# Attention and two feed-forward layers on one core: other places for the weight conversions in attention, and less filler a unit up to unit 34

## The chip, the core and the metric

The kernel runs on one core of a Trainium2 chip. The core has TensorE (PE: products into PSUM; its weight loads are shown as PEld), VectorE (DVE), ScalarE (ACT), GpSimd (POOL) and SyncE (SP, which issues most of the transfers). Each engine works through its own instructions in their order, and waits on semaphores for the others. The metric is the time of one execution in microseconds (us), the median of several.

## The reference, cut to what matters

```python
# attention: q, k, v are (4, 8, 576, 64), s is (4, 8, 576)
scores = scale * q @ k.T
bias = minimum(-(cum[:, None] - cum[None, :]), 0)       # cum: running sum of max(s, 0)
attn = softmax(where(causal, -1e9, scores + bias))
x = attn @ v                                            # then as (2304, 512)
# first layer: w_in (512, 2048), w_out (2048, 512)
h = x @ w_in ;  x = (h * sigmoid(1.702 * h)) @ w_out
# second layer, weights of its own
h = x @ w_in ;  x = (P(h) / (Q(h) + 1e-6)) @ w_out      # P, Q: polynomials of h and |h|
```

[...]

## The kernel before, in words

**Attention** is cut into 80 units: 4 batches, 4 pairs of heads, 5 blocks of 128 query rows. Unit j has batch j // 20, pair (j % 20) // 5 and block (0, 1, 4, 2, 3)[j % 5]; in the names of the rows, s_3_0 is pair 3, block 0. A unit makes its scores on PE for two heads (L251), adds the mask and takes the row minimum on DVE (L285), the exponential on ACT (L292), the reciprocal of the sums on DVE (L300, L301), and scales the rows on POOL (L304). Two or three units later PE transposes them (L323 to L344), ACT or DVE copies them out of PSUM (L348, L351), and PE multiplies with the values (L370). The first two units of a pair also prepare the next pair: transposes (L218), copies on ACT (L176), differences on DVE (L179).

**Filler.** Between these pieces PE gets pieces of the first layer, for one batch at a time (mlp1_first), over the first 5 of the 16 blocks f of the hidden dimension: first products h (L563), their activation (L574, L575, L577, L580), and then second products a (L587), which sum over all 5 blocks f. How much is given to a unit is set by FILL / 20 in planned microseconds. A piece of 6 products is planned at 0.74. The filler of batch 0 opens at unit 23, that of batch 1 at unit 43, that of batch 2 at unit 63; before unit 23 there is none, and a unit gets only a product or so on idle data (L75).

**Conversions.** A weight block is half of an f: half 0 from w_in, half 1 from w_out. Below, c0 to c4 are half 0 of f = 0 to 4, and c5 to c9 half 1 of them; CONV_J says after which unit each is put out. Six more, p0 to p5, for f = 5, 6, 7, are put out after the units AHEAD_J and parked in DRAM. One conversion is a transfer of 512 KB (L493 or L495 on SP), two ACT instructions (L497, L499), three on DVE (L500, L501, L502), an addition on POOL (L504), the high part on ACT (L505), and the low part on POOL (L506); PE multiplies with both parts. The transferred words lie in a slot of the tile stgA: up to unit 23 always slot 2, then slots 0, 1, 2 in turn (staging; `self.stg_free = j > 23`). A transfer waits until the conversion before it in its slot is past L504.

**Order.** PE's order is written out by hand, as the code says it. For the other engines a planner with costs of its own sets the order inside the limits that the code gives (`behind`: not before the exponential and the reciprocal of unit j). After attention come the rest of the first layer and the second layer; the change moves nothing there.

Of the kernel before, what the change touches and what calls it, by code (L numbers as in the profile page):

```python
# [40 lines left out]
EARLY = tuple(range(3, 40, 5))  # L41
PACE = 0.5
AHEAD_F = (5, 6, 7)
AHEAD_J = (35, 39, 43, 47, 51, 55)
FILL = 33.0
AHEAD, AHEAD_0 = 2, 3
COPY_V = ((0, 0), (0, 4))
W2_SLOTS = 7
CONV_J = (9, 12, 15, 18, 20, 22, 24, 26, 28, 30)
CONV = [(f, 0) for f in range(F1)] + [(f, 1) for f in range(F1)]  # L50
STG = 1536
BT_BUFS, G_BUFS = 7, 9
# [3 lines left out]
class Fused:  # L56
# [340 lines left out]
    def attention(self, att, mlp):  # L397
        units = [(b, p, t) for b in range(NB) for p in range(NP) for t in (0, 1, 4, 2, 3)]
        n = len(units)
        self.pairs, self.state = {}, {}  # L400
        self.filler, self.credit = iter(()), 0.0
        self.n_bt = 0
        self.cold, self.idle_bank = True, self.bank("T", "idle")
        self.warm(10)
        nprep = iter(())
        self.sums_load(att)
        ld = self.pair_load(att, 0, 0, True)
        self.sums(att)
        for _ in self.prep(att, 0, 0, ld, True):
            pass  # L410
        start = ld["values"]
        ld = self.pair_load(att, 0, 1)
        start()
        ld["values"]()
        self.store_sums()
        done = 0
        for j in range(n + AHEAD + 1):
            i = max(j - (AHEAD_0 if j < 20 else AHEAD), -1)
            for e in range(done, i):
                for _ in self.unit_transpose(att, units[e]):  # L420
                    pass
                self.unit_values(att, units[e - 1])
            done, k = i + 1, i - 1
            self.stg_free = j > 23
            tr = iter(())
            if j < n:
                b, p, t = units[j]
                idx = j % 5
                if idx == 0 and units[j][1:] != (NP - 1, 0) or (idx == 0 and b + 1 < NB):
                    nprep = self.prep(att, *divmod(b * NP + p + 1, NP), ld)  # L430
            if i >= 0 and i < n and units[i][0] and i % 20 == 1:
                self.filler = chain(self.filler, self.mlp1_first(mlp, units[i][0] - 1))
                self.cold = False
            q = FILL / 20
            if j < n:
                self.unit_scores(att, units[j], 0)
                if j:
                    next(nprep, None)
            self.fill(q / 3, 1)
            if 0 <= i < n:  # L440
                tr = self.unit_transpose(att, units[i])
                next(tr, None)
            if j < n:
                self.unit_scores(att, units[j], 1)
            self.fill(q / 3, j < 4)
            for _ in tr:
                pass
            if j < n and idx == 4:
                for _ in nprep:
                    pass  # L450
                g = b * NP + p + 2
                if g < NB * NP:
                    ld = self.pair_load(att, *divmod(g, NP))
                    ld["values"]()
            if k >= 0:
                self.unit_values(att, units[k])
            self.fill(q / 3, j < 4)
            if j == AHEAD_J[0]:
                self.stg_n, self.stg_k = 0, 2
                buf = self.stg_slot[:, 2 * STG : 2 * STG + 1024].bitcast(F32R)  # L460
                buf = buf.rearrange("p (i f) -> p i f", i=2)
                self.queue = [
                    lambda f=f, half=half: self.park(buf, 1, f, half)
                    for f in AHEAD_F for half in range(2)
                ]
            if j in COEF_J:
                with self.behind(self.tail):
                    if j == COEF_J[0]:
                        self.coefficients()
                    else:  # L470
                        self.nc.scalar.activation(self.cf[:, 6:8], self.cf[:, 4:6], AF.Abs)
            if j in CONV_J or j in AHEAD_J:
                with self.behind(self.tail):
                    self.emit(1)
        for _ in self.filler:
            pass
# [446 lines left out]
```

## Time and profile before

| | |
|---|---|
| median of 3 runs | 1057.89 us (1056.5 to 1062.92) |
| the profiled execution | 1063.09 us, its span 1061.3 us |
| PE busy | 1030.1 us, 97% of the span |
| DVE, ACT, POOL busy | 804.8, 724.1, 315.7 us |
| attention | the first 327 us or so |

The page gives busy times and groups of instructions for the whole span; further views give the same for a stretch, the instructions in order of time, and what each waited for. A "gap" below is idle time of an engine just before an instruction; the arrow names what ended it. PE's ends are modelled, so PE shown as busy may still be slow; its clock is in the windows' rows (1.00 is full speed, 0.50 half).

### The profile page before, as it was taken

What the parts mean: (1) busy time and instruction counts of PE and PEld (TensorE: products, weight loads), DVE (VectorE), ACT (ScalarE), POOL (GpSimd) and SP (SyncE); (2) the same over time, 40 slices, a digit from 0 to 9 for tenths busy, and PEclk for the clock granted to TensorE, in tenths of its full rate; (3) what the DMA queues carried; (4) which work ended last, traced back from release to release, by engine and by line L of the source; (5) the groups of instructions that cost most, each with busy time, mean ns of one, the idle gap of its engine ahead of it and who ended that gap; (6) DMA issues with size and microseconds to landing.
All of it is one profiled execution on the core that took longest, in us unless ns stands there. A gap on an engine that the chain in (4) does not pass through costs nothing.

```text
span 1061.3 us, 19897 instructions
## 1 busy us (share of the span) xinstructions
PE 1030.1 (97%) x7073; PEld 944.9 (89%) x7073; DVE 804.8 (76%) x1874; ACT 724.1 (68%) x1668; POOL 315.7 (30%) x421
## 2 busy tenths in 40 slices
PE   7998999999999899989999999999999999999997
PEld 4766898898999899889999999998999999999996
DVE  6777867766644999786388444898998988989886
ACT  6788978977855675554265234788787777777765
POOL 4445835543420003231001211222222222222222
PEclk8899999999999999999999999999999999999999
DMA  8446465543215648897136546000010010100000
GB/s 183 117 120 171 122 163 146 144 136 84 50 48 223 204 141 285 273 285 246 46 124 209 196 123 241 31 30 31 1 48 13 17 44 1 33 29 1 31 1 30
DMA packets 79755, 117.31 MB, mean 111 GB/s; under 512 B 25728, under 2 KB 63616, under 8 KB 78060
## 3 DMA queue, kind: packets, MB, share of 16 engines
q1 hardware_dynamic: 73288, 96.55, 31.3%
q0 software_dynamic: 6144, 19.19, 5.0%
q8 instruction: 56, 0.92, 0.4%
q14 instruction: 43, 0.35, 0.1%
q10 hardware_dynamic: 224, 0.30, 0.1%
HBM read 75.08 MB, written 32.05 MB: 101 GB/s over the span
## 4 chain that ended last, share of the span: by engine, by line
PE 80%; DMA 7%; ACT 5%; DVE 4%; issue 3%; POOL 1%; SPq 0%; ACTq 0%; POOLq 0%; DVEq 0%
PE h L563 32%; PE a L739 18%; PE a L587 14%; PE s L251 5%; PE O L370 5%; DMA raw<-in_moe_w_out_dram 4%; PE tp L344 3%; DMA stgA<-in_moe_w_in_dram 1%; PE idle L75 1%; DMA raw<-in_moe_w_in_dram 1%; ACT cvx L499 1%; ACT kh L176 1%; PE tk L218 1%; POOL wd L543 1%; DVE cvx L504 1%
## 5 line engine op out<-in xcount | busy, mean ns | idle before, releaser
L563 PE MATMUL h<-x,u 128*128 128x288 f32 x1536 | 233.0, 298 | 7.6 <-DVE g L575 3.8
L587 PE MATMUL a<-gh,u 128*128 128x288 f32 x1024 | 229.8, 299 | 2.3 <-ACT gh L577 2.3
L563 PEld LDWEIGHTS h<-x,u 128*128 128x128 f32 x1536 | 213.0, 189 | 12.6 <-DVE g L575 4.3
L722 POOL TENSOR_TENSOR gl<-u,gh 128x384 fp32r<-128x384 f32 x96 | 105.5, 1099 | 290.3 <-ACT gh L720 261.1
L587 PEld LDWEIGHTS a<-gh,u 128*128 128x128 f32 x1024 | 172.1, 189 | 6.6 <-ACT gh L577 2.5
L563 PE MATMUL h<-y,u 128*128 128x384 f32 x864 | 165.7, 336 | 0.0
L563 PEld LDWEIGHTS h<-y,u 128*128 128x128 f32 x864 | 152.9, 188 | 6.2
L587 PE MATMUL a<-gl,u 128*128 128x288 f32 x512 | 147.7, 295 | 1.0 <-DVE gl L580 1.0
L739 PE MATMUL a<-u,gh 128*128 128x512 f32 x432 | 114.6, 394 | 0.9 <-ACT gh L720 0.9
L304 POOL TENSOR_SCALAR bt<-bt,sm 128x128 f32<-128x128 f32 (+3 forms) x129 | 72.0, 569 | 112.4 <-DVE sm L301 58.0
L574 ACT ACTIVATE g<-h 128x288 f32<-128x288 f32 x128 | 51.4, 406 | 74.7 <-PE h L563 64.3
L648 POOL DMA_DIRECT2D x<-xp x64 | 35.4, 554 | 224.4 <-DVE g L575 95.6
L587 PEld LDWEIGHTS a<-gl,u 128*128 128x128 f32 x512 | 96.3, 188 | 2.1 <-DVE gl L580 1.6
L292 ACT ACTIVATE bt<-bt,mn 128x128 f32<-128x128 f32 (+3 forms) x129 | 74.8, 580 | 29.2 <-DVE mn L285 27.2
L739 PEld LDWEIGHTS a<-u,gh 128*128 128x128 f32 x432 | 80.0, 188 | 14.9 <-ACT gh L720 1.8
L575 DVE SCALAR_TENSOR_TENSOR g<-g,h 128x288 f32<-128x288 f32 x128 | 57.0, 449 | 45.3 <-ACT g L574 44.9
L285 DVE CUSTOM_DVE_ANT_0 bt<-s,mask 128x128 f32<-128x128 f32 (+3 forms) x129 | 62.3, 483 | 36.8 <-PE s L251 30.9
L720 ACT ACTIVATE gh<-u 128x384 fp32r<-128x384 f32 x96 | 50.6, 527 | 57.7 <-DVE u L718 57.6
L251 PE MATMUL s<-k 68*128 68x256 f32 (+2 forms) x192 | 73.4, 387 | 7.3 <-ACT k L176 4.1
L705 ACT ACTIVATE y<-h,cf 128x384 f32<-128x384 f32 x96 | 55.4, 577 | 33.8 <-PE h L563 33.8
L710 DVE SCALAR_TENSOR_TENSOR y<-s,cf,y 128x384 f32<-128x384 f32 x96 | 59.3, 618 | 20.4 <-ACT s L707 19.1
L577 ACT ACTIVATE gh<-g 128x288 fp32r<-128x288 f32 x128 | 55.5, 440 | 28.3 <-DVE g L575 27.4
(117 smaller groups left out, 2112.2 us busy)
## 6 DMA issues: line engine op xcount, KB each, us to landing
raw<-in_moe_w_in_dram SPq DMA_DIRECT2D x24, 512.0 KB
raw<-in_moe_w_out_dram SPq DMA_DIRECT2D x24, 512.0 KB
x<-xp POOLq DMA_DIRECT2D x64, 144.0 KB, 3.1
wd<-park POOLq DMA_DIRECT2D x36, 256.0 KB, 4.5
u<-wd SPq DMA_DIRECT2D x8, 1024.0 KB
x2p<-st SPq DMA_DIRECT2D x32, 144.0 KB
xp<-x2p SPq DMA_DIRECT2D x32, 144.0 KB
xp<-x SPq DMA_DIRECT2D x32, 144.0 KB
```

Of the source, the lines that this page charges most:

```text
L251: nc.tensor.matmul(sc[: c1 - c0, :w], lhsT=q[:, c0:c1], rhs=k[:, j0 : j0 + w], start=m == 0, stop=m == 1,)
L285: nc.vector.tensor_tensor_reduce(bt[:, j0 : j0 + w], sc[:, :w], mask, 1.0, 3.0e38 if i == 0 else mn[:, 0:1], ALU.add, ALU.min, mn[:, i : i ...
L292: ex = nc.scalar.activation(bt[:, :n], bt[:, :n], AF.Exp, bias=mn[:, i : i + 1], scale=-1.0, accum_out=sm[:, col : col + 1],)
L304: nc.gpsimd.tensor_scalar(bt[:, :n], bt[:, :n], inv[:, i : i + 1], 1.0, ALU.mult, ALU.mult)
L563: nc.tensor.matmul(ps_tile, lhsT=u[:, wl, kk * P : (kk + 1) * P], rhs=x(xl, kk), start=(n == 0), stop=(n == 3 * KD - 1),)
L575: nc.vector.scalar_tensor_tensor(g[:, :w], g[:, :w], 1.0, h, ALU.add, ALU.mult)
L577: nc.scalar.activation(gh[:, :w], g[:, :w], AF.Copy)
L587: nc.tensor.matmul(acc, lhsT=u[:, wl, d * P : (d + 1) * P], rhs=g[gl], start=(first and i == 0), stop=(last and i == 2),)
L705: nc.scalar.activation(y, h, AF.Abs, scale=cf[:, 4:5])
L710: nc.vector.scalar_tensor_tensor(y, s, cf[:, 7:8], y, ALU.mult, ALU.add)
L722: nc.gpsimd.tensor_tensor(gl, p, gh.bitcast(F32), ALU.subtract)
L739: nc.tensor.matmul(accs[m], lhsT=g[gl][:, m * P : (m + 1) * P], rhs=u[:, wl, :], start=(f == 0 and i == 0), stop=(f == NF - 1 and i == 2),)
```

## The change

Three tables of numbers change. CONV_J puts the ten conversions of attention at units 8 to 34 where they were at 9 to 30, four and three units apart and then two to three; five of them now fall before unit 23, where six did. AHEAD_J puts each of the six parked ones three units later. FILL_1 gives each unit before unit 35 25/20 = 1.25 planned us of filler in place of 33/20 = 1.65; from unit 35 on it is 1.65 as before. The work is the same, and the order after unit 62 too.

```diff
-AHEAD_J = (35, 39, 43, 47, 51, 55)
-FILL = 33.0
+AHEAD_J = (38, 42, 46, 50, 54, 58)
+FILL, FILL_1 = 33.0, 25.0
...
-CONV_J = (9, 12, 15, 18, 20, 22, 24, 26, 28, 30)
+CONV_J = (8, 12, 16, 19, 22, 25, 28, 30, 32, 34)
...
-            q = FILL / 20
+            q = (FILL_1 if j < 35 else FILL) / 20
```

**SP, units 18 to 21.** The transfers of c3 (the first L493 of each piece below) and c4 (the second), and what stands around them: vn are the values of the pair after the next, kn and qn its keys and queries, k and kh copies of the prepared ones, L495 halves from w_out. Before:

```order
L225 DMA k_0_861<-qs_0_860 64x1152
L493 DMA stgA<-in_moe_w_in_dram 128x4x256
L152 DMA vn_0_840<-in_v_dram 128x4x64 x2
L156 DMA vn_0_840<-in_v_dram 64x2x64
L204 DMA k_1_1120<-rows 4x2304
L145 DMA kn_3_1745<-in_k_dram 96x2x384
L495 DMA stgA<-in_moe_w_out_dram 128x1024
L145 DMA qn_3_1747<-in_q_dram 96x2x384
L225 DMA kh_1_1118<-kh_1_1118 64x1152
L493 DMA stgA<-in_moe_w_in_dram 128x4x256
```

And of the change:

```order
L225 DMA k_0_861<-qs_0_860 64x1152
L152 DMA vn_0_840<-in_v_dram 128x4x64 x2
L156 DMA vn_0_840<-in_v_dram 64x2x64
L493 DMA stgA<-in_moe_w_in_dram 128x4x256
L204 DMA k_1_1120<-rows 4x2304
L145 DMA kn_3_1700<-in_k_dram 96x2x384
L495 DMA stgA<-in_moe_w_out_dram 128x1024
L145 DMA qn_3_1702<-in_q_dram 96x2x384
L225 DMA kh_1_1118<-kh_1_1118 64x1152
L495 DMA stgA<-in_moe_w_out_dram 128x1024
L493 DMA stgA<-in_moe_w_in_dram 128x4x256
```

The transfer of c3 moved behind the three transfers of vn; that of c4 behind one more L495.

**POOL, units 24 to 26.** L304 scales attention's rows (bt), L580 belongs to the filler, L504 and L506 to conversions c5 and c6. Before:

```order
L580 TENSOR_TENSOR gl<-g,gh 128x288
L504 TENSOR_TENSOR stgA<-stgA 128x512 x2
L506 TENSOR_TENSOR u_1_769<-stgA,u_1_769 128x512
L580 TENSOR_TENSOR gl<-g,gh 128x288
L304 TENSOR_SCALAR bt_1_0_0_1414<-bt_1_0_0_1414,sm_1_0_1413 128x128
L304 TENSOR_SCALAR bt_1_0_1_1461<-bt_1_0_1_1461,sm_1_0_1413 128x128
L506 TENSOR_TENSOR u_0_606<-stgA,u_0_606 128x512
```

And of the change:

```order
L304 TENSOR_SCALAR bt_1_0_0_1389<-bt_1_0_0_1389,sm_1_0_1388 128x128
L304 TENSOR_SCALAR bt_1_0_1_1423<-bt_1_0_1_1423,sm_1_0_1388 128x128
L580 TENSOR_TENSOR gl<-g,gh 128x288
L504 TENSOR_TENSOR stgA<-stgA 128x512
L304 TENSOR_SCALAR bt_1_1_0_1483<-bt_1_1_0_1483,sm_1_1_1482 128x256
L304 TENSOR_SCALAR bt_1_1_1_1514<-bt_1_1_1_1514,sm_1_1_1482 128x256
L506 TENSOR_TENSOR u_0_568<-stgA,u_0_568 128x512
```

Before, two conversions stood there together; now one does, and c6 follows three units later.

**PE and ACT, unit 35 of the change.** The last conversion, c9, writes the tile u_4; a are second products. PE:

```order
L344 MATMUL tp_2_2_1_2102<-ident,bt_2_2_1_1959 128x128 x3
L370 MATMUL O_2_0_1977<-pt_2_4_2001,vn_2_1363 64x64 x10
L587 MATMUL a_0_2034<-gh,u_4_1268 128x288
L587 MATMUL a_0_2034<-gl,u_4_1268 128x288
L587 MATMUL a_0_2034<-gh,u_4_1268 128x288
```

ACT, where O is what PE's L370 above writes:

```order
L292 ACTIVATE bt_3_0_1_2091,sm_3_0_2050<-bt_3_0_1_2091,mn_3_0_1_2092 128x128
L380 ACTIVATE x_79<-O_2_0_1977 128x256
L176 ACTIVATE kh_0_2058<-tk_0_1_2070 64x288
L380 ACTIVATE x_79<-O_2_0_1977 128x64
L505 ACTIVATE u_4_1268<-stgA 128x512
```

Before, L505 of c9 stood on ACT in unit 31, ahead of the exponential of unit 32, and PE's three products with that tile in unit 32. Now L505 stands in unit 35 behind two copies of O, and the products right behind the O that these copies read.

## Rows read from the trace of the kernel before

**Rows 1.** The page, busy us (share of the span) and instructions of each engine.

```profile
PE 1030.1 (97%) x7073; PEld 944.9 (89%) x7073; DVE 804.8 (76%) x1874; ACT 724.1 (68%) x1668; POOL 315.7 (30%) x421
```

**Rows 2.** Windows: units 10-22, 23-34, 63-74; filler stream. Columns in the first line.

```profile
core 0: us, PE busy (x) PEld busy (x) DVE busy (x) ACT busy (x) POOL busy (x), PEclk, DMA share, GB/s
42.20:86.83 44.63, 40.69 (x362) 31.08 (x360) 36.04 (x131) 38.38 (x107) 23.45 (x33) 0.92 0.59 158
86.83:141.59 54.76, 51.41 (x435) 44.97 (x433) 40.00 (x126) 46.19 (x124) 36.34 (x44) 1.00 0.49 126
253.56:303.21 49.65, 49.65 (x435) 44.82 (x433) 30.07 (x109) 37.80 (x106) 19.71 (x32) 1.00 0.25 56
500.00:520.00 20.00, 20.00 (x153) 20.00 (x153) 7.30 (x17) 5.56 (x14) 2.16 (x4) 1.00 0.22 68
```

**Rows 3.** Windows of single units without filler: units 12, 17 and 22.

```profile
49.05:53.81 4.76, 4.76 (x33) 3.82 (x29) 3.54 (x12) 3.41 (x9) 2.90 (x6) 0.64 0.88 229
64.02:68.87 4.85, 3.32 (x33) 2.64 (x30) 2.41 (x10) 2.75 (x8) 0.88 (x3) 1.00 0.45 114
83.83:86.83 3.00, 2.98 (x29) 2.16 (x27) 2.11 (x8) 2.48 (x7) 1.25 (x4) 1.00 0.96 293
```

**Rows 4.** Windows of unit 26 and of its twin in batch 3, unit 66.

```profile
101.22:108.70 7.48, 5.36 (x45) 4.12 (x43) 7.32 (x20) 6.81 (x20) 4.74 (x5) 1.00 0.63 175
265.93:270.30 4.37, 4.37 (x44) 4.03 (x42) 3.84 (x13) 4.27 (x16) 1.50 (x3) 1.00 0.32 69
```

**Rows 5.** Timeline of PE: start, us, what; in brackets the gap and its releaser.

```profile
47.73 0.52 PE L344 MATMUL tp<-ident,bt 128*128 128x128 f32 x3 [1.21 <-ACT pt L348]
...
104.52 0.63 PE L344 MATMUL tp<-ident,bt 128*128 128x128 f32 x4 [1.23 <-DVE g L575]
```

**Rows 6.** Timeline of ACT: the first instruction of c2, c3 and c5.

```profile
66.26 0.65 ACT L497 ACTIVATE stgA<-stgA 128x512 int32<-128x512 uint32 x1 [2.06 <-DMA stgA<-in_moe_w_in_dram]
...
76.23 0.68 ACT L497 ACTIVATE stgA<-stgA 128x512 int32<-128x512 uint32 x1
...
96.37 0.66 ACT L497 ACTIVATE stgA<-stgA 128x512 int32<-128x512 uint32 x1 [0.56 <-DMA stgA<-in_moe_w_out_dram]
```

**Rows 7.** Timeline of SP's queue: transfers of c2, c3, vn and c5.

```profile
60.29 0.38 SPq L493 DMA_DIRECT2D stgA<-in_moe_w_in_dram  x1
...
70.94 0.39 SPq L493 DMA_DIRECT2D stgA<-in_moe_w_in_dram  x1
73.64 2.00 SPq L152 DMA_DIRECT2D vn<-in_v_dram  x2
75.69 0.67 SPq L156 DMA_DIRECT2D vn<-in_v_dram  x1
...
92.69 0.35 SPq L495 DMA_DIRECT2D stgA<-in_moe_w_out_dram  x1
```

**Rows 8.** Timeline of POOL and DVE where c5 and c6 meet.

```profile
101.93 1.43 POOL L504 TENSOR_TENSOR stgA<-stgA 128x512 int32<-128x512 int32 x1 [0.96 <-DVE stgA L502]
...
102.14 1.51 DVE L501 TENSOR_SCALAR stgA<-stgA 128x512 int32<-128x512 int32 x1
```

**Rows 9.** Timeline around the end of c9 (L505, L506) and its first use.

```profile
130.59 0.73 ACT L176 ACTIVATE qs<-tq 64x288 fp32r<-64x288 f32 x2
131.21 0.61 ACT L505 ACTIVATE u<-stgA 128x512 fp32r<-128x512 f32 x1
...
132.05 1.28 POOL L506 TENSOR_TENSOR u<-stgA,u 128x512 fp32r<-128x512 f32 x1
...
133.74 0.38 ACT L380 ACTIVATE x<-O 128x256 fp32r<-128x256 f32 x1 [0.15 <-PE O L370]
...
133.99 0.30 PE L587 MATMUL a<-gh,u 128*128 128x288 f32 x1
```

**Rows 10.** Instructions on the tile stgA: ns min/median/max, first and last start.

```profile
L497 ACT ACTIVATE stgA<-stgA x16: 643/665/689, 43.5 to 227.4; 128x512 int32<-128x512 uint32 x16
...
L501 DVE TENSOR_SCALAR stgA<-stgA x16: 416/427/1506, 45.7 to 230.0; 128x512 int32<-128x512 int32 x16
```

## The prediction

> **What bounds the kernel now.** The page comes first: PE is busy for 97% of the span [rows 1], so only a stretch where PE idles or runs slowly has anything to give. The windows show which. From unit 23 to unit 34 batch 1 takes 54.76 us; batch 3 does the same attention and filler, with no conversion beside it, in 49.65 us, all of it with PE busy [rows 2]. So the conversions c4 to c9 cost that stretch 5.1 us, and without them PE bounds it. Of the 5.1, unit 26 alone has 7.48 - 4.37 = 3.11 [rows 4], where PE waits for DVE [rows 5]. Before unit 23 there is no filler to cover a wait: PE is busy for 40.69 of 44.63 us at a mean clock of 0.92, and ACT for 38.38 [rows 2]. Single units show the price. Unit 22 takes 3.00 us; unit 12, with the same block of rows, takes 4.76 at a granted clock of 0.64, a mean of the levels 2.4 and 1.2 GHz, right behind a gap of 1.21 us on PE [rows 3, 5]. Unit 17, the same block again, takes 4.85, because ACT waits 2.06 us for the transfer of c2 [rows 3, 6]. All that the change moves lies ahead of unit 63; what follows shifts with it, one for one.
>
> **The change, part by part.** Nothing is added or removed, so each term is a wait that goes or comes.
>
> *c0, one unit earlier.* Its words are long there. It goes from blocks 3 and 0 to blocks 2 and 3, which have fewer ACT instructions since no pair is prepared. The gap of 1.21 us in unit 11 and the slow unit 12 behind it (4.76 - 3.00 = 1.76) make 2.97 us [rows 3, 5]. ACT is busy for 86% of this stretch [rows 2], so part of c0's ACT time still shows: I take **-2.5** between 0 and -3.0.
>
> *c1 and c2* keep their places on ACT. c2's transfer is still issued behind the transfers ahead of it on SP, so its wait of 2.06 us stays: **0**.
>
> *c3, one unit later, and behind vn on SP.* Before, its transfer was issued at 70.94, and ACT took up c3 at 76.23 with no wait [rows 6, 7]. Now it comes behind the three transfers of vn, which go out from 73.64, when PE has read the old values, to 75.69 + 0.67 = 76.36 [rows 7]. From issue to ACT's start took 66.26 - 60.29 = 5.97 us for c2, and 96.37 - 92.69 = 3.68 for c5, both ended by the landing [rows 6, 7]. So the words land at 80.0 to 82.3 on the old time line. ACT arrives after one more exponential, about 0.7 long (76.9). It waits 3.1 to 5.4 us; behind it stand the copies of the next pair's keys and the copies of transposes that PE needs. c2's wait of 2.06 made unit 17 1.85 longer, 0.9 for each us [rows 3, 6]. That gives 2.8 to 4.9: **+3.8**. Below, it is 0 if the values are read earlier; above, a half clock as in unit 12 adds 1.8: 6.7.
>
> *c4 and the head of the filler.* Of the 5.1 us in units 23 to 34, 2.0 are not in unit 26, and most of these lie where c4 meets the first filler. With c4 alone there and less filler I take **-1.5**, between 0 and -2.0.
>
> *c5 and c6 apart.* They met because c5 still used slot 2 while c6 took slot 0 at once; now c5 has slot 0, three units ahead of c6. Unit 26's 3.11 us is the bound. One conversion still passes there: **-2.1**, between 0 and -3.1. Part of it shows on DVE: L501 took 1.51 us there, and 0.43 in the median, while L504 of the other conversion ran on POOL [rows 8, 10]. The Trainium skill (SBUF — State Buffer, section "SBUF: two separate sides") says that the two engines hold a shared pair of ports by turns, each for a whole instruction; the row agrees. By that rule L304 and L580 of POOL block DVE as well, which the change does not remove; if all of unit 26 were that, this term would be 0 and the sum 2.1 higher.
>
> *Less filler.* Each of the 12 units from 23 to 34 gets 0.4 planned us less, 4.8 in all; a piece of 6 products, planned at 0.74, takes 6 x 20/153 = 0.78 us [rows 2], so 5.1 us of PE work moves to units 35 to 43. By the plan's prices a batch has 29.6 us of filler. Before, it ran out in unit 40, and units 41 and 42 had none; now 15.0 go by unit 34 and the rest ends in unit 43, and batch 1's ends in unit 61, still before unit 63. PE does the same work in the same units 23 to 62, and no idle unit is filled, since 41 and 42 only ran shorter: 0. But ACT's work in units 23 to 34 is 46.19 us [rows 2] and hardly shrinks, since the activations move only within that stretch, while PE needs 49.65 - 5.1 = 44.6. ACT then bounds it, by up to 46.19 - 44.6 = 1.6 us, lost later on PE: **+1.0**, between 0 and 1.6.
>
> *c9 and the second products.* Before, c9's last part ended at 132.05 + 1.28 = 133.33, and the product that reads it started at 133.99: 0.66 us to spare [rows 9]. Now L505 stands behind two copies of O on ACT, and PE's product right behind that O. From the end of O: the copy 0.38, the copy of keys 0.73 / 2 = 0.37, the second copy, with a quarter of the columns, 0.25 at a guess from these, L505 0.61, then L506 1.28 [rows 9], in sum 2.9; two products (0.26) run between, hand-overs add some 0.2. **+2.8**, PE idle. Below, 0 if PE arrives late for another reason; above, 4.2, if L504 (1.43) [rows 8] is late as well. Behind PE wait the scores of unit 36 and all its engines.
>
> *Parked ones.* p0 to p5 keep their four units, beside filler, as c7 to c9 did inside the 2.0 above: 0, give or take 1.
>
> **Sum:** -2.5 + 3.8 - 1.5 - 2.1 + 1.0 + 2.8 = **+1.5 us**. Against the profiled execution (1063.1; span 1061.3) that is 1064.6. It stands 5.2 above the median of the runs, 1057.9; the runs differ by 6.4, so I put the difference on the median: **1059.4 us**, no measurable change (a measurement of this kernel can tell about 1%, 10.6 us).
>
> **The rivals.**
> *The waits that go are not replaced* (faster). c3's words land in time, or PE has enough transposes ahead, and c9's parts are ready since ACT is less crowded. For it: c7 to c9 cost nearly nothing in filled units. Against it: SP's and ACT's orders as printed. -2.5 - 1.5 - 2.1 + 1.0 = -5.1, with the full gains -8.1: 1050 to 1053. Chance 0.27.
>
> *c3 holds c4 up too* (slower). c4 uses the same slot, so its transfer waits for c3's L504. If c3's words land later than about 81.5, 4.6 us behind ACT's arrival, PE idles for over 4 us with no filler, its clock falls as in unit 12, and c4 comes late to the first filler. c3 then costs 4.9 + 1.8 = 6.7 in place of 3.8, c4 gives nothing: +2.9 + 1.5 on top, 1063.8. For it: the gap of 1.21 us was followed by a clock of 0.64 [rows 3, 5]; against: no clock fell behind the gap of 1.23 in unit 26, where there is filler. The Trainium skill (TensorE: Matmul & The Clock Gate, "What's actually happening") has the clock halved where the array has been idle; unit 12 agrees. Chance 0.25.
>
> *The spacing does nothing* (the change does not do what it says): ACT is the bound of these units however the conversions lie, and what one unit saves another loses: 1058. For it: ACT's 86% [rows 2]. Chance 0.10.
>
> **How the numbers follow.** The forecast, gains and new waits about even, has 0.38. The range goes from the full gains without new waits (1057.9 - 8.1 = 1049.8) to the slower rival with c9's upper end (1063.8 + 1.4) and the spread of the runs (some 3): **1049 to 1068**. Faster by over 1% (below 1047.3) needs the full gains and more: 0.06. Slower by over 1% (above 1068.5) needs all upper ends: 0.09. Within 1%: 0.85.
>
> **What would show it.** Right, if in the new trace ACT's first instruction of c3 has a gap of 3 to 5 us that a transfer ends, unit 35 has a PE gap of 2 to 3 us ahead of the products with f = 4, unit 26 is near 4.4 us, units 11 and 12 have neither gap nor half clock, and unit 63 starts within 5 us of 253.56. Wrong at c3, if that gap is under 1 us; wrong at c9, if PE does not idle there; wrong on the filler, if units 23 to 34 take over 51 us without such gaps, or if ACT is not nearly full there.

## The result and the profile after

The changed kernel takes 1068.08 us (median of 9 runs, 1066.67 to 1073.5); the kernel before, on the same chips, 1059.92 (9 runs, 1056.5 to 1063.99). The ratio is 1.0077, with a 95% interval of 1.0057 to 1.0097: about 8 us **slower**. The forecast was no change, 1059.4; the median lies 0.08 us above the upper end of its range (1068). Two executions of one experiment below (all conversions done by unit 30) took 1656 us at a mean clock of 0.556, and are left out of its median and ratio.

The profiled execution of the changed kernel took 1073.5 us (span 1071.7), 5.4 above the median, so single stretches of it are read with care and sizes are taken from the runs. The page, against [rows 1]:

```profile
PE 1034.1 (96%) x7073; PEld 948.0 (88%) x7073; DVE 808.8 (75%) x1874; ACT 723.5 (68%) x1668; POOL 314.8 (29%) x421
```

Same work, PE a little longer. Unit 63 starts at 262.84 where it was 253.56, and behind it every unit takes what it took. So 9.28 of the 10.4 us between the two traces (spans 1071.7 and 1061.3) lie ahead of unit 63. Windows of the changed kernel (columns as in [rows 2]): units 10 to 22, units 23 to 34, units 35 to 42; then units 12, 21 and 26, and two stretches at half clock.

```profile
43.20:91.36 48.16, 41.33 (x362) 30.76 (x360) 36.91 (x133) 37.83 (x107) 23.99 (x34) 0.93 0.61 157
91.36:139.81 48.45, 45.93 (x399) 40.04 (x398) 40.37 (x121) 43.18 (x121) 30.43 (x39) 1.00 0.41 105
139.81:181.58 41.77, 37.57 (x320) 34.18 (x319) 24.08 (x81) 27.75 (x77) 15.92 (x23) 0.92 0.49 139
50.42:53.60 3.18, 3.18 (x34) 2.69 (x30) 2.54 (x11) 3.00 (x9) 2.57 (x6) 1.00 0.98 251
79.20:87.57 8.37, 5.40 (x35) 3.72 (x32) 6.63 (x19) 7.98 (x24) 3.05 (x4) 0.73 0.64 177
102.94:108.26 5.32, 4.19 (x39) 3.29 (x37) 4.68 (x13) 4.99 (x16) 2.98 (x4) 1.00 0.41 112
83.05:89.87 6.82, 5.74 (x29) 4.20 (x28) 5.05 (x17) 5.08 (x16) 3.28 (x4) 0.50 0.78 215
147.90:154.72 6.82, 6.50 (x30) 6.49 (x31) 2.86 (x9) 3.27 (x9) 0.27 (x1) 0.50 0.40 133
```

And units 35 to 42, and unit 21, of the kernel before:

```profile
141.59:172.17 30.58, 30.58 (x294) 27.65 (x292) 22.28 (x75) 25.16 (x73) 13.11 (x18) 1.00 0.56 154
...
79.91:83.83 3.92, 3.42 (x36) 2.62 (x32) 3.76 (x15) 3.82 (x13) 3.29 (x4) 1.00 0.93 290
```

Units 23 to 34 got shorter, 48.45 for 54.76, as less filler would have it. Units 35 to 42 got longer by 11.2. Of that 3.5 are the filler that moved, since the same stretch takes 34.07 where only the filler is changed (below); the other 7.7 lie in units 35 and 36. Unit 21 takes 8.37 where it took 3.92. By stretches, after minus before, from the starts of the units:

| units | forecast | traces | what is seen there |
|---|---|---|---|
| 0 to 10 | 0 | +1.0 | a half clock from 28.43 to 35.26, ahead of all that moved; before, from 29.13 to 32.54 |
| 11 to 22 | -2.5 + 3.8 = +1.3 | +3.5 | c3's wait, and a half clock behind it |
| 23 to 42 | -1.5 - 2.1 + 1.0 + 2.8 = +0.2 | +4.9 | PE waits for c9, and a half clock behind it |
| 43 to 62 | 0 | -0.1 | the parked conversions cost nothing |

**c3.** ACT's first instructions of c2, c3 and c4 in the changed kernel, against [rows 6]:

```profile
67.33 0.67 ACT L497 ACTIVATE stgA<-stgA 128x512 int32<-128x512 uint32 x1 [2.46 <-DMA stgA<-in_moe_w_in_dram]
...
79.47 0.66 ACT L497 ACTIVATE stgA<-stgA 128x512 int32<-128x512 uint32 x1 [3.34 <-DMA stgA<-in_moe_w_in_dram]
...
92.16 0.69 ACT L497 ACTIVATE stgA<-stgA 128x512 int32<-128x512 uint32 x1
```

And SP's queue, against [rows 7]:

```profile
72.22 2.04 SPq L152 DMA_DIRECT2D vn<-in_v_dram  x2
74.30 0.67 SPq L156 DMA_DIRECT2D vn<-in_v_dram  x1
75.08 0.53 SPq L493 DMA_DIRECT2D stgA<-in_moe_w_in_dram  x1
```

The third transfer is c3's, right behind vn; 4.4 us later ACT takes up the words (the 64-bit weights of a block, read as pairs of 32-bit integers), after a wait of 3.34, inside the forecast's 3.1 to 5.4. What the middle of the term left out is the clock: it is 0.50 from 83.05 to 89.87. PE itself idled for no more than 1.69 us at a time in unit 21:

```profile
81.39 0.47 PE L218 MATMUL tq<-ident,qn 96*128 96x96 f32 x3 [1.69 <-DVE mn L285]
```

c4 starts with no wait for its words.

**c9.** PE in unit 35 of the changed kernel, against [rows 9]:

```profile
142.54 0.95 PE L370 MATMUL O<-pt,vn 128*64 128x64 f32 x20
146.76 0.40 PE L587 MATMUL a<-gh,u 128*128 128x288 f32 x1 [3.28 <-ACT u L505]
...
148.22 0.85 PE L587 MATMUL a<-gh,u 128*128 128x288 f32 x2 [0.92 <-POOL u L506]
```

ACT there, and POOL and DVE ahead of the wait of 0.88:

```profile
144.26 0.37 ACT L380 ACTIVATE x<-O 128x256 fp32r<-128x256 f32 x1
144.66 0.43 ACT L176 ACTIVATE kh<-tk 64x288 fp32r<-64x288 f32 x1
145.97 0.22 ACT L380 ACTIVATE x<-O 128x64 fp32r<-128x64 f32 x1 [0.88 <-DVE x L381]
146.09 0.62 ACT L505 ACTIVATE u<-stgA 128x512 fp32r<-128x512 f32 x1
```

```profile
144.17 1.28 POOL L504 TENSOR_TENSOR stgA<-stgA 128x512 int32<-128x512 int32 x1 [0.75 <-ACT pt L348]
...
144.45 1.03 DVE L300 TENSOR_SCALAR sm<-sm 128x2 f32<-128x2 f32 x1
145.51 0.42 DVE L381 TENSOR_TENSOR x<-O,x 128x256 fp32r<-128x256 f32 x1
```

The order is the one forecast: L505 behind both copies of O, the products behind L505 and L506. The two gaps are 4.2 us where 2.8 were forecast. ACT takes up the first copy 0.77 us after the last O (143.49 to 144.26), with other work in between. c9's own L504 runs on POOL from 144.17 to 145.45, and L505 could not have begun before its end. It begins 0.64 us later still, since ACT's second copy waits 0.88 for DVE's L381, which stands behind an L300 of 1.03 us on two columns, beside that same L504 (last section). Then the clock is 0.50 from 147.90 to 154.72, which the term did not hold at all. Units 35 and 36 take 16.47 us here, and 9.70 before with six more second products.

### The profile page after: what moved, and what is told of

Same layout as the page of the kernel before. It is cut to its first block, busy times and chain, and to the rows that moved or that the text cites. A ratio compares the mean times of both kernels' runs of the same rounds, so it can differ in the third digit from the quotient of the medians.

```text
span 1071.7 us, 19895 instructions
## 1 busy us (share of the span) xinstructions
PE 1034.1 (96%) x7073; PEld 948.0 (88%) x7073; DVE 808.8 (75%) x1874; ACT 723.5 (68%) x1668; POOL 314.8 (29%) x421
## 4 chain that ended last, share of the span: by engine, by line
PE 78%; DMA 9%; DVE 4%; ACT 4%; issue 3%; POOL 1%; SPq 1%; ACTq 0%; DVEq 0%; POOLq 0%
PE h L563 31%; PE a L739 18%; PE a L587 13%; PE s L251 5%; PE O L370 5%; DMA raw<-in_moe_w_out_dram 4%; PE tp L344 3%; DMA raw<-in_moe_w_in_dram 3%; DMA stgA<-in_moe_w_in_dram 1%; ACT cvx L499 1%; ACT raw L497 1%; PE tk L218 1%; POOL wd L543 1%; PE tp L323 1%; DMA k<-qs 1%
## 5 line engine op out<-in xcount | busy, mean ns | idle before, releaser
L304 POOL TENSOR_SCALAR bt<-bt,sm 128x128 f32<-128x128 f32 (+3 forms) x129 | 71.6, 566 | 120.8 <-DVE sm L301 62.2
```

What stands on the lines that cost most here:

```text
L304: nc.gpsimd.tensor_scalar(bt[:, :n], bt[:, :n], inv[:, i : i + 1], 1.0, ALU.mult, ALU.mult)
```

## The experiments

Ratios are to the kernel before, run beside each experiment on the same chip; "changed" is 1.0077. Edits are to the changed kernel where nothing else is said. A difference of two ratios carries about 0.0027, or 3 us, either way (the two intervals taken together, an estimate); what is smaller is not told from noise.

### c9 earlier

```diff
-CONV_J = (8, 12, 16, 19, 22, 25, 28, 30, 32, 34)
+CONV_J = (8, 12, 16, 19, 22, 25, 28, 30, 31, 32)
```

> The changed kernel with the last two conversions of attention put out at units 31 and 32 in place of 32 and 34; all else as changed. Theory (waits and clock): the second products of unit 35 then find c9 ready, the gaps of 3.28 and 0.92 us on PE go and so does the half clock of 6.8 us behind them (3.4 us): 7.6 us less than the changed kernel, so about 1060.5, a ratio to the kernel before of 1.000 (0.997 to 1.003); unit 35 takes 5 to 6 us. Rival (the filler that moved is the loss): no change, ratio 1.008, and units 35 to 42 still take near 41 us. Rival (only the wait counts, the clock falls for another reason): 4.2 us less, ratio 1.004.

Measured: 1064.77 us, ratio 1.0056 (1.0036 to 1.0077). A **miss** for the theory's 1.000: 0.0021 better than changed, with intervals that overlap. PE no longer waits for L505, but units 35 and 36 still take 12.61. First the window, then POOL and PE:

```profile
136.93:149.54 12.61, 10.91 (x92) 9.40 (x91) 8.54 (x29) 9.42 (x30) 7.85 (x11) 0.86 0.47 124
```

```profile
136.91 1.30 POOL L504 TENSOR_TENSOR stgA<-stgA 128x512 int32<-128x512 int32 x1 [1.94 <-DVE sm L300]
138.18 1.26 POOL L506 TENSOR_TENSOR u<-stgA,u 128x512 fp32r<-128x512 f32 x1
139.41 0.79 POOL L580 TENSOR_TENSOR gl<-g,gh 128x288 fp32r<-128x288 f32 x1
140.18 2.48 POOL L304 TENSOR_SCALAR bt<-bt,sm 128x384 f32<-128x384 f32 x4
```

```profile
139.49 0.40 PE L587 MATMUL a<-gh,u 128*128 128x288 f32 x1 [0.77 <-DVE sm L300]
140.82 0.55 PE L344 MATMUL tp<-ident,bt 128*128 128x128 f32 x3 [0.92 <-POOL bt L304]
```

With c8 and c9 one unit apart, their POOL parts fall together (L504 is c9's, L506 c8's), ahead of the rows (L304) that PE wants to transpose. A half clock follows here too, from 141.57 to 144.98. One wait has taken the place of another.

### c3 back

```diff
-CONV_J = (8, 12, 16, 19, 22, 25, 28, 30, 32, 34)
+CONV_J = (8, 12, 15, 18, 22, 25, 28, 30, 32, 34)
```

> The changed kernel with c2 and c3 put out at units 15 and 18, as before the change; the transfer of c3 is then issued ahead of vn again. Theory (waits and clock): ACT's wait of 3.34 us for c3 and the half clock of 6.8 us behind it go; unit 21 takes about 4 us in place of 8.4, so 4 to 7 us less than the changed kernel: about 1062.5, ratio 1.001 to 1.004. Rival (c3's wait only takes the place of another, ACT being full up to unit 23): ratio 1.007 to 1.008, and unit 23 still starts near 91. c9's gaps in unit 35 stay by both.

Measured: 1063.25, ratio 1.0029 (1.0011 to 1.0047): 0.0048, or 5.1 us (2.2 to 8.0), better than changed, as the theory had it. The edit moves c2 as well, so this is the price of the two places together. SP and then ACT at c3, unit 21 behind them, and units 35 and 36:

```profile
68.12 0.39 SPq L493 DMA_DIRECT2D stgA<-in_moe_w_in_dram  x1
70.81 0.94 SPq L152 DMA_DIRECT2D vn<-in_v_dram  x2
```

```profile
74.52 0.68 ACT L497 ACTIVATE stgA<-stgA 128x512 int32<-128x512 uint32 x1
```

```profile
78.36:82.18 3.82, 3.28 (x35) 2.58 (x31) 3.67 (x15) 3.75 (x12) 3.31 (x4) 1.00 0.94 296
133.91:150.25 16.34, 12.14 (x93) 11.04 (x91) 9.61 (x28) 9.81 (x28) 7.38 (x10) 0.79 0.46 132
```

With the transfer ahead of vn, ACT has no wait for c3 and unit 21 no loss. This execution has a half clock of its own earlier, from 66.63 to 73.46, behind c2's wait, so the size is taken from the runs. c9's price stays whole, with its half clock (0.79 is the mean of both units): the two losses are separate.

### The filler alone

Against the kernel before:

```diff
-FILL = 33.0
+FILL, FILL_1 = 33.0, 25.0
...
-            q = FILL / 20
+            q = (FILL_1 if j < 35 else FILL) / 20
```

> The kernel before with the one change that units up to 34 get 1.25 planned us of filler in place of 1.65; the conversions and the parked ones as before. Theory (waits and clock): PE does the same work later; units 23 to 34 get shorter by up to 5 us, units 35 to 43 longer by as much; 1060 to 1061.5, ratio 1.000 to 1.002. Rival (the filler that moved is the loss, since ACT and DVE are too full beside it later): ratio 1.005 to 1.008, with gaps on PE in units 35 to 43.

Measured: 1059.96, ratio 0.9999 (0.9984 to 1.0014). The rival is out. Windows: units 23 to 34, 35 and 36, 35 to 42; then units 11 and 12.

```profile
82.78:135.97 53.19, 48.23 (x399) 41.50 (x398) 41.78 (x125) 46.19 (x125) 35.62 (x44) 0.97 0.50 125
135.97:144.74 8.77, 8.77 (x93) 8.13 (x91) 6.89 (x24) 8.06 (x25) 2.08 (x4) 1.00 0.44 119
135.97:170.04 34.07, 34.07 (x320) 31.14 (x319) 23.68 (x82) 26.58 (x75) 14.05 (x21) 1.00 0.62 172
```

```profile
42.99:50.46 7.47, 6.23 (x68) 5.19 (x67) 7.22 (x26) 6.71 (x22) 5.33 (x8) 1.00 0.59 160
```

Two things are to be seen. Units 23 to 34 lost 36 products (435 to 399), some 4.7 us by the 20/153 of [rows 2], and are 1.6 shorter, where a half clock of 3.4 us (the 0.97) took up to 1.7; units 35 to 42 grew by 3.5. The filler went later, and little else. And units 11 and 12, with c0 still at unit 9, take 7.47 here with no half clock, against 9.08 before. The gap ahead of unit 12 is there (1.18 us), the half clock behind it is not: the slow unit 12 of [rows 3] was not a property of that order.

### PE kept busy while it waits for c9

```diff
             if k >= 0:
                 self.unit_values(att, units[k])
+            if j == 35:
+                self.idle_bank = self.bank("T", "idle2")
+                self.warm(15)
```

> The changed kernel with 15 more products on idle data put into PE's order in unit 35, ahead of the second products that wait for c9, so that PE does not idle through that wait (they take about 2 us if PE has nothing else to do). It tells the price of the half clock apart from that of the wait. Theory (waits and clock): the wait stays, the half clock behind it goes, 3 to 3.4 us less than the changed kernel: 1064.7, ratio 1.004 to 1.005. Rival (the clock falls there whatever PE did, or costs nothing since PE was waiting for others): ratio 1.008; if the added products come late and only add work, 1.009 to 1.010.

Measured: 1065.79, ratio 1.0058 (1.0038 to 1.0078): 0.0019, 2.0 us, less than changed, which is within the noise. The ratio lies between the theory's 1.004 to 1.005, inside the interval, and the rival's 1.008, just outside. In the trace the added products take 3.41 us, not about 2 (lines are 3 higher behind the edit):

```profile
143.36 3.41 PE L75 MATMUL idle<-mask 128*128 128x512 bf16 x14
146.75 0.41 PE L590 MATMUL a<-gh,u 128*128 128x288 f32 x1
...
148.19 0.53 PE L590 MATMUL a<-gh,u 128*128 128x288 f32 x2 [0.91 <-POOL u L509]
```

```profile
139.78:153.27 13.49, 12.53 (x107) 9.59 (x106) 9.45 (x28) 9.28 (x28) 6.60 (x9) 1.00 0.53 153
```

The products that read c9 start when they did (146.75 for 146.76), so the wait is the same; but the clock stays at 1.00, and units 35 and 36 take 13.49 in place of 16.47. Of what c9 costs, the clock is 3.0 us in this pair of traces; the runs, with 2.0, do not contradict it and do not show it by themselves. The Trainium skill (TensorE: Matmul & The Clock Gate, "What's actually happening") has the clock halved where the array has been idle; here it fell where PE idled, in two traces, and did not where PE was given idle data, in this trace and the next experiment's, so the traces agree.

### Both waits kept busy

The last edit, and in unit 21:

```diff
                 self.unit_scores(att, units[j], 0)
+                if j == 21:
+                    self.warm(8)
...
                 self.unit_scores(att, units[j], 1)
+                if j == 21:
+                    self.warm(4)
```

> The changed kernel with products on idle data in both places where PE idles: 12 in unit 21, beside ACT's wait for c3, and 15 in unit 35, ahead of the second products that wait for c9. The waits stay; only PE's idling goes. Theory (waits and clock): no half clock behind either wait, unit 21 takes 5 to 6 us in place of 8.4 and units 35 and 36 13.5 in place of 16.5; 1062 to 1063.5, ratio 1.002 to 1.004, so half or more of the loss is the clock. Rival (the clock behind c3's wait costs nothing, since ACT bounds these units): ratio 1.0055 to 1.006, as with the products in unit 35 alone.

Measured: 1063.55, ratio 1.0050 (1.0029 to 1.0071). **Inconclusive**: it lies between the two expectations. In the traces, units 21 and 22 take 9.92 at a clock of 1.00 for 12.13 in the kernel of the last experiment, but that execution, at 1069.03 the longest of the seven, had half clocks earlier, in units 11, 12, 18 and 19. The clock's share in c3's price is not settled.

### c0 alone

Against the kernel before:

```diff
-CONV_J = (9, 12, 15, 18, 20, 22, 24, 26, 28, 30)
+CONV_J = (8, 12, 15, 18, 20, 22, 24, 26, 28, 30)
```

> The kernel before with c0 put out at unit 8 in place of 9, and nothing else. The forecast's term: units 11 and 12 take 2 to 2.5 us less than the 9.1 of before; ratio 0.998. Rival (the half clock in unit 12 came by the run's luck, and the gap of 1.21 us goes only by half): units 11 and 12 take 7.9 us where the clock is full, as in the changed kernel, and in runs without that half clock nothing is gained over before: ratio 0.999 to 1.000.

Measured: 1060.68, ratio 1.0005 (0.9986 to 1.0025). The term of -2.5 us (0.9976) lies outside. Units 11 and 12:

```profile
44.27:52.15 7.88, 6.95 (x68) 5.24 (x67) 7.14 (x28) 7.11 (x22) 5.16 (x8) 1.00 0.73 204
```

That is 0.4 longer than the 7.47 with c0 at unit 9 and a full clock. The forecast took a half clock of one execution for the price of a place.

### Both cured, with the last two conversions one unit apart

```diff
-CONV_J = (8, 12, 16, 19, 22, 25, 28, 30, 32, 34)
+CONV_J = (8, 12, 15, 18, 22, 25, 28, 30, 31, 32)
```

> The changed kernel with both of the two edits tried alone so far: c2 and c3 put out at units 15 and 18 (c3's transfer ahead of vn), c8 and c9 at 31 and 32. Theory (waits and clock, the two are all of the loss that is left): their gains add up, 2.2 and 5 us by the ratios, so ratio 1.0077 - 0.0048 - 0.0021 = 1.001 (0.999 to 1.003); unit 35 still takes some 8 us, since POOL's second part of c9 stands ahead of the rows that PE transposes there. Rival (one hides behind the other): ratio 1.003 to 1.005.

Measured: 1064.13, ratio 1.0043 (1.0016 to 1.0070). This is in the rival's range, and the theory's 1.001 lies outside; but that 1.001 is itself a sum of three measured ratios, so whether the edits add up is not settled. Units 23 to 34 take 48.81 us, unit 35 still 8.60, by the same collision on POOL as with c9 earlier.

### All conversions done by unit 30

First with the changed filler, and then with the full one as well (the last two lines):

```diff
-CONV_J = (8, 12, 16, 19, 22, 25, 28, 30, 32, 34)
+CONV_J = (8, 12, 15, 18, 22, 25, 27, 28, 29, 30)
...
-FILL, FILL_1 = 33.0, 25.0
+FILL, FILL_1 = 33.0, 33.0
```

> The changed kernel's filler and parked conversions, c0 at 8, c4 at 22 and c5 at 25 as changed, but c2 and c3 at 15 and 18 and c6 to c9 at 27, 28, 29, 30, so that c9 is done three units ahead of unit 35. Theory (waits and clock): the gains of the change are kept (c0, c4, and c5 apart from c6) and neither wait is there; unit 35 near 4.7 us as with the filler alone, unit 63 starts 2 us ahead of that kernel's 251.3; 1057 to 1059, ratio 0.997 to 0.999. Rival (four conversions in four units fill ACT and DVE and cost what the two waits cost): ratio 1.001 to 1.004, with gaps on PE in units 27 to 32.

> The same places of the conversions as in the run that ends them at 30 (c0 at 8, c2 and c3 at 15 and 18, c4 at 22, c5 at 25, c6 to c9 at 27 to 30), the parked ones as changed, but with 1.65 planned us of filler a unit from unit 23 on as before the change. By the theory that less filler is worth nothing by itself: within 0.002 of the ratio of that run. Rival (with full filler the second products begin in unit 32 and wait for c9, whose last part stands in unit 31): gaps of 1 to 3 us on PE in units 32 to 34, ratio 0.002 to 0.004 higher.

Measured: 1064.00, ratio 1.0038 (1.0019 to 1.0057), and 1061.94, ratio 1.0011 (0.9993 to 1.0030). The **rival** was right for the first. Units 35 and 36 take 8.76 with no gap, so c9 in time costs nothing there; but unit 31 takes 10.58:

```profile
115.57:126.15 10.58, 7.30 (x44) 5.95 (x43) 9.81 (x24) 8.67 (x23) 10.58 (x11) 0.71 0.52 137
136.93:145.69 8.76, 8.76 (x92) 8.12 (x91) 6.65 (x25) 7.07 (x24) 2.09 (x4) 1.00 0.46 119
```

```profile
120.87 0.58 PE L251 MATMUL s<-k 68*128 68x256 f32 x1 [2.46 <-DVE k L179]
```

POOL is busy for the whole of it, DVE's differences (L179) of the next pair's keys are late for PE, and the clock is 0.50 from 120.03 on. With full filler the same unit took 8.78 us at full clock, and the rival's wait does not show: PE has no gap over 0.4 us in units 32 to 34. The two ratios differ by 0.0027, the wrong way for the rival and more than the 0.002 of the theory; that is at the edge of the noise, and stays open.

### The second products later

```diff
-FILL, FILL_1 = 33.0, 25.0
+FILL, FILL_1 = 33.0, 22.0
...
-CONV_J = (8, 12, 16, 19, 22, 25, 28, 30, 32, 34)
+CONV_J = (8, 12, 15, 18, 22, 25, 28, 30, 32, 34)
...
-            q = (FILL_1 if j < 35 else FILL) / 20
+            q = (FILL_1 if j < 36 else 38.0 if j < 43 else FILL) / 20
```

> The changed kernel with c2 and c3 at units 15 and 18, all other conversions as changed (c9 at 34), and the filler cut to 1.10 planned us a unit up to unit 35 and raised to 1.90 in units 36 to 42, so that the second products begin in unit 36 and the ones that read c9 come some two units later. Theory (waits and clock): no gap behind L505 or L506 any more; units 35 and 36 take 8 to 9.5 us together; unit 43 starts near 168 to 170; ratio 0.997 to 1.000. Rival (the conversions cost PE the same wherever they lie, and what the spacing saves up to unit 34 is lost to ACT and DVE behind it): ratio 1.002 to 1.004.

Measured: 1059.18, ratio 0.9992 (0.9974 to 1.0011). Against c3 back, which has the same places of the conversions, it is 0.0037 (3.9 us, 1.2 to 6.6) faster. c9's L505 now ends at 140.84 and L506 at 142.21; PE's first product that reads c9 starts at 141.82 and the one that needs L506 at 142.26, just in time, since products that read other tiles fill units 35 and 36:

```profile
140.92 1.29 POOL L506 TENSOR_TENSOR u<-stgA,u 128x512 fp32r<-128x512 f32 x1 [1.34 <-ACT u L505]
```

```profile
142.26 0.53 PE L587 MATMUL a<-gh,u 128*128 128x288 f32 x2
```

Units 23 to 34, then 35 and 36:

```profile
85.93:131.83 45.90, 43.85 (x382) 37.44 (x380) 37.36 (x120) 42.16 (x116) 29.87 (x38) 1.00 0.52 123
131.83:141.18 9.35, 9.07 (x92) 8.19 (x90) 8.39 (x25) 9.23 (x28) 7.58 (x10) 1.00 0.53 145
```

The whole loss is gone, with c9 at unit 34 as in the change, and nothing is gained over the kernel before. The cure changes how the filler is spread, so the 3.9 us hold that as well.

### Even steps of two units

```diff
-CONV_J = (8, 12, 16, 19, 22, 25, 28, 30, 32, 34)
+CONV_J = (8, 12, 15, 18, 21, 24, 26, 28, 30, 32)
```

> The changed kernel's filler and parked conversions with the ten conversions at units 8, 12, 15, 18, 21, 24, 26, 28, 30, 32: c3's transfer ahead of vn, c5 and c6 apart, two units from one to the next at the end, c9 two units earlier than changed. Theory (waits and clock): units 23 to 34 near 48.8 us as where c6 to c9 lay at 28, 30, 31, 32, and c9 done before unit 35, so that unit 35 takes 4.7 to 6 us; ratio 0.997 to 1.000. Rival (POOL's second part of c9 still stands ahead of the rows that PE transposes in unit 35, as with c8 and c9 at 31 and 32): unit 35 takes 8 us or more, ratio 1.002 to 1.004.

Measured: 1060.25, ratio 1.0009 (0.9988 to 1.0030). Units 35 and 36 are clean, as expected, and unit 35 takes 4.71 us where the rival had 8 or more. The loss is gone. Units 23 to 34 are 50.11, not 48.8:

```profile
85.21:135.32 50.11, 46.91 (x399) 40.00 (x398) 41.85 (x125) 45.84 (x124) 34.12 (x43) 1.00 0.53 126
135.32:144.09 8.77, 8.77 (x93) 8.13 (x91) 6.92 (x25) 7.69 (x25) 3.63 (x7) 1.00 0.59 171
```

No version beat the kernel before by more than a measurement can tell.

## Why the prediction was wrong

The two new waits stood where it put them; the sum failed on both sides. With c3 back and the second products later the ratio is 0.9992, so what is left of the change is worth -0.8 us (-2.8 to +1.2), where the terms for it (c0, c4, c5 and c6 apart, filler) gave -5.1. Even steps, which keep the change's own filler and have neither wait, give +1.0 (-1.3 to +3.2). And the two waits cost 5.1 + 3.9 = 9.0 by the runs, where they were put at 3.8 + 2.8 = 6.6. So 4.3 us were lost on gains that did not come, and 2.4 on waits that cost more: together the 6.7 between +1.5 and +8.2.

- **c0: -2.5, measured +0.5 (-1.5 to +2.7).** This step failed most. Of its 2.97 us, 1.76 was the half clock of unit 12, taken from a single execution; a kernel with c0 at the same place had none there. The gap of 1.21 went to 0.56, yet unit 11, where c0's L505 and L506 now stand, got longer, 4.69 for 4.32; which of its instructions did that is not shown.
- **c3: +3.8, measured 5.1** (2.2 to 8.0, c2's place with it). SP's order and the wait (3.34) were read right. The half clock was in the bounds (6.7), and the middle was taken without it. The rival "c3 holds c4 up too" had the half clock, but not its way there: PE's longest gap was 1.69 us, not over 4, and c4 found its words there.
- **c4, c5 and c6 apart: -3.6, seen -1.3 to -1.6.** In units 23 to 34 the step looked right: against the filler alone they fall from 53.19 (51.5 without its half clock) to 48.45, and unit 26 to 5.32 (4.4 expected, and 4.44 where c3 is back). But c9 had left these units for 35, and the last part of c8 too (L506 at 139.96), and took their price with them; with c9 two units earlier (even steps) the stretch takes 50.11. Where all ten conversions are done in time and neither wait is there, units 23 to 62, with the same work, take 165.1 and 165.5 us (second products later, even steps) for 166.7 before. The step took the gain of a stretch for a gain of the whole.
- **Less filler: +1.0, measured -0.1 (-1.7 to +1.5).** By the noise it may be anything in its bounds, 0 to 1.6. That ACT bounds units 23 to 34 did not come about: in the changed kernel ACT is busy for 43.18 of 48.45 us there, PE for 45.93; with the filler alone ACT has 46.19, as the term said, but in 53.19 us.
- **c9: +2.8, measured 3.9** (1.2 to 6.6, against a kernel whose second products come later). The order was right, the gaps 4.2, the upper end, and for the most part by its reason: L504 ended at 145.45, about 1.0 us after the copies would have been done by the term (143.49 + 1.0). The other 0.6 came from ACT's late first copy and DVE's L300, which the term did not have. The half clock behind them (3.0 us by the traces with and without products on idle data) was left out, though the term itself said that PE idles there for some 3 us; unit 12 was at hand as a warning that had been booked as c0's gain.
- **Parked ones: 0, seen -0.1** in units 43 to 62, which take 81.26 us both in the changed kernel and with the filler alone, where the parked ones stand as before. Right.
- **The range** ended at 1068. It lay too low since its slow end still counted -2.5 for c0 and -2.1 for c5 and c6, and had no half clock behind c9.

## What to carry to other kernels

A planned wait of PE is priced with what comes behind it: 4.2 us of idling in unit 35 brought 6.8 us at half clock in both traces that had it, so idle products in the hole are worth trying where the wait cannot go. A slow stretch in one profiled execution counts as removable only if another execution of the same order shows it too. And before the steps of a chain are spread, look whether its last step still ends ahead of its first reader: moving the last step close to the one before it only exchanged its wait for a collision, while moving the reader two units later, or spacing the last steps by two units, cured it.

## What was not expected of the hardware

A DVE instruction on two columns can take as long as a POOL instruction beside it. In the changed kernel, DVE and then POOL:

```profile
99.78 1.21 DVE L300 TENSOR_SCALAR sm<-sm 128x2 f32<-128x2 f32 x1 [0.30 <-ACT bt L292]
```

```profile
99.67 1.29 POOL L506 TENSOR_TENSOR u<-stgA,u 128x512 fp32r<-128x512 f32 x1
```

Without POOL's part beside it the same instruction took 0.15 (at 136.76, with c9 earlier). DVE's ends with POOL's, 100.99 and 100.96. It is no single case: of the 80 instructions of this line in the changed kernel, 13 took over 0.4 us, each ending within 0.04 us of the end of a POOL instruction, and the 52 with none beside them took 0.17 at most. So a conversion can also lengthen small steps of attention that stand beside it, which no busy time of the conversion shows. The Trainium skill (SBUF — State Buffer, "SBUF: two separate sides") has GpSimd and a VectorE instruction in a two-port mode, or with two inputs in SBUF, hold a shared pair of ports by turns, the first to start for its whole instruction. These rows agree as to the turns; no run shows the mode of the DVE instruction.
